# Decoding two cached-attention and MLP layers: the last wo behind the last V, the next K in quarters of chunks, and idle products on TensorE

## The chip, the core and the metric

One core of a Trainium2 chip runs the kernel in one launch. The metric is device time in microseconds (us), the median of several executions. All data is float32, and the caches and weights come from HBM in each execution: 286.14 MB.

## What is computed

One token (D = 512) goes through attention with a cache, an MLP, and both once more with the same weights and caches:

```python
def _A_ref(x, k_cache, v_cache, wq, wo):          # 32 heads, 4096 keys, 128 wide
    q = (x @ wq).reshape(B, Sq, H, Dh).transpose(0, 2, 1, 3)
    scores = jnp.einsum("bhqd,bhkd->bhqk", q, k_cache) * (Dh ** -0.5)
    p = _softmax(scores, axis=-1)
    o = jnp.einsum("bhqk,bhkd->bhqd", p, v_cache)
    return o.transpose(0, 2, 1, 3).reshape(B, Sq, H * Dh) @ wo
def _B_ref(x, w1, b1, w2, b2):                    # F = 1376
    return jnp.einsum("bsf,fd->bsd", _gelu(jnp.einsum("bsd,df->bsf", x, w1) + b1), w2) + b2
x = x + _A_ref(_layernorm(x, axis=-1), A_k_cache, A_v_cache, A_wq, A_wo)
x = x + _B_ref(_layernorm(x, axis=-1), B_w1, B_b1, B_w2, B_b2)
# and these two lines once more
```

## The kernel before

The 32 heads are worked in G = 8 groups of J = 4. A group's K and its V are 8.39 MB each, cut into C = 8 chunks of NC = 2048 elements per partition; a chunk is four quarters of U = 512, one for each head of the group. All of it lives in one array in SBUF, the arena, at places that the code names: A_AT (0), C_AT (8 NC) and B_AT (16 NC) hold a K or a V each (B_AT's last chunk and a half is used otherwise), SHARED (10 U) and PAIR (8 U) hold weights, SCRATCH one tile.

A group runs through these steps. `scores` (L184): TensorE (PE) multiplies the query with the eight chunks of K into pS. `exponentials` (L189): VectorE (DVE) finds the maximum, ScalarE (ACT) does the exponential. `weights` (L200) turns the result, `values` (L214) multiplies with the eight chunks of V into pO, `head_out` (L219) multiplies with wo, and `next_queries` (L301) makes the next group's queries with wq. The layer's norm is folded in, so queries don't wait for it.

Layer 1 takes the groups 0 to 7. Layer 2 goes back from 7 to 0, since the last group's K and V are still in the arena: K of group 7 in C_AT, V of group 7 in A_AT, and 26 of the 32 quarters of group 6's V in B_AT. The other six quarters were copied to PSUM (pK, L328) and are copied back by ACT in the change of layers (L375). Group 6's K is loaded again during that change, into whatever comes free (`begin_k`, L352): one chunk in SHARED, one in PAIR, two in C_AT behind the scores of chunks 0 and 1, four in C_AT behind those of chunks 2 to 5. `pair` (L364), one load of wq for the next group and wo for group 6, takes C_AT + 6 NC to the end of C_AT, wq first. From n = 2 on (L386), `homes` gives each K and V a third of the arena in turn. The V of n = 2 goes to C_AT in two pieces, chunks 0 to 5 and chunks 6 and 7 (L394).

All loads of weights and caches are issued by one queue, SP, in the order of the code (L70), each when the engines are done with what it overwrites. PE's products are kept in the order of the code too (L74). In a layer's last group V comes in four pieces (LAST: chunks 0 to 3, 4 and 5, 6, 7), its wo is loaded ahead of them to PAIR (L321, L393), and w1 and w2 follow in pieces. `mlp` (L240) multiplies with the four rows of w1, does the gelu on DVE and ACT (L254 to L263) and multiplies with the eleven rows of w2 (L264), piece by piece as they land. In the change of layers w1 and w2 share one place, so w2's pieces wait for PE's products with w1; after the last layer they lie in A_AT and wait for nothing there.

Of the kernel before, what the change touches and what calls it, by code (L numbers as in the profile page):

```python
# [17 lines left out]
P = 128  # L18
# [32 lines left out]
def decode_layers(ctx: ExitStack, tc: tile.TileContext, x, k, v, w, w1, b1, w2, b2, out):  # L51
# [5 lines left out]
    def ctile(name, *shape):  # L57
        return const.tile([P, *shape], F32, name=name)
# [6 lines left out]
    def at(first, n):  # L65
        return arena[:, first : first + n]

    def load(first, src):
        t = at(first, src.shape[-1])
        tc.keep_in_program_order(nc.sync.dma_start(t, src))  # L70
        return t

    def matmul(*a, **kw):
        tc.keep_in_program_order(nc.tensor.matmul(*a, **kw))  # L74

    def quarters(first):
        return [at(first + U * j, U) for j in range(4)]

    def part(src, g, a, b):
        return src[g][:, NC * a : NC * b]  # L80

    def of_w(row, i, n):
        return w[row][:, NC * i : NC * (i + n)]

    def by_four(t):
        return t.rearrange("p (j n) -> p j n", j=4)
# [13 lines left out]
    power = ctile("power", 1)  # L100
    nc.gpsimd.memset(power, -0.5)


    pS, pO = (psum.tile([P, 512], F32, name=n) for n in ("pS", "pO"))
    pK = [psum.tile([P, 512], F32, name=f"pK{i}") for i in range(6)]
# [8 lines left out]
    def of_32(t, n, i=0):  # L114
        return t[:, : 32 * n].rearrange("p (c q) -> p c q", q=32)[:, :, i]
# [12 lines left out]
    def turned(src, wide=False):  # L128

        t = work.tile([P, P], F32, name="turned")  # L130
        if wide:
            for j in range(J):
                q = slice(32 * j, 32 * j + 32)
                nc.vector.transpose(t[q], src[q, P * j : P * (j + 1)])  # L134
        else:
            nc.vector.transpose(t, src[:, :P])
        return t

    def set_x(xin0, scale, xin1, queries=True):
        s = small("x_sum")  # L140
        t = x_wide if queries else small("x1", 8)
        if not queries:
            nc.gpsimd.memset(pairs(t)[:, :, 1], 1.0)
        x = pairs(t)[:, :, 0]
        nc.vector.scalar_tensor_tensor(x, xin0, scale, xin1, op0=ALU.mult, op1=ALU.add, accum_out=s)  # L145
        if queries:
            for j in range(1, J):
                nc.gpsimd.tensor_copy(pairs(t[:, 32 * j :])[:, :, 0], x)
        return t, s

    def minus_mean(s, at):
        for j in range(J):
# [31 lines left out]
    def scores(z, c, kt):  # L184
        for j in range(J):
            matmul(pS[32 * j : 32 * j + C, :], z[:, j, C - 1 - c : 2 * C - 1 - c], kt[j],
                   start=(c == 0), stop=(c == C - 1))
# [26 lines left out]
    def values(i, pt, vt, c):  # L214
        for j in range(J):
            matmul(pO[32 * j : 32 * j + 4, :], pt[:, j, c, :], vt[j],
                   start=(i == 0), stop=(i == C - 1))
# [19 lines left out]
                matmul(pO, on[:, d : d + P], wt[:, d, :], start=(d == 0), stop=(d == 3))  # L237
        return of_32(turned(pS) if last else turned(pO, wide=True), 4)

    def mlp(xs, s, w1_t, w2_t, load_w2=None):  # L240
        xb = small("xb", 4)
        nc.gpsimd.tensor_tensor(xb, pairs(xs)[:, :, 0], b2c, op=ALU.add)  # L242
        for c in range(4):
            for j in range(J):
                matmul(pO[32 * j : 32 * j + 2, :FJ], pairs(xs)[:, c, :], w1_t[c][:, FJ * j : FJ * (j + 1)],
                       start=(c == 0), stop=(c == 3))
            if c == 0:
                nm, ss = mean_of(xs, s)
            if c == 1:
                r = rstd_of(ss)  # L250
            if load_w2 and c < 3:
                load_w2(c)
        ht = at(SCRATCH, 32 * FB)
        nc.vector.transpose(ht, pO[:, : 32 * FB])  # L254
        h, u, a, z, t, g = (small(f"gelu_{i}", FB) for i in "huaztg")
        nc.vector.scalar_tensor_tensor(h, of_32(ht, FB, 1), nm, of_32(ht, FB), op0=ALU.mult, op1=ALU.add)
        if load_w2:
            load_w2(3)
        nc.vector.scalar_tensor_tensor(u, h, r, b1c, op0=ALU.mult, op1=ALU.add)
        nc.vector.scalar_tensor_tensor(a, u, 0.044715, u, op0=ALU.mult, op1=ALU.mult)  # L260
        nc.vector.scalar_tensor_tensor(z, a, 1.0, u, op0=ALU.add, op1=ALU.mult)
        nc.scalar.activation(t, z, AF.Tanh, scale=float(np.sqrt(2.0 / np.pi)))
        nc.vector.scalar_tensor_tensor(g, t, 1.0, u, op0=ALU.add, op1=ALU.mult)  # L263
        for c in range(FB):  # L264
            for j in range(J):
                matmul(pS[32 * j : 32 * j + 1, :P], g[:, c : c + 1], w2_t[c][:, P * j : P * (j + 1)],
                       start=(c == 0), stop=(c == FB - 1))
        return of_32(turned(pS), 4), xb

    def load_w1(first, a, b):  # L270
# [2 lines left out]
    def load_w2(first, a, b):  # L273
        load(first + U * a, w2[:, U * a : U * b])

    def in_rows(first, n, rows):
        return [at(first + n * i, n) for i in range(rows)]
# [4 lines left out]
            for c in range(a, b):  # L282
                yield c, quarters(home + NC * c)

    zero = ctile("zero", 4)
    nc.vector.memset(zero, 0.0)
    xs, s = set_x(zero, 1.0, xcol)

    def first_queries(xs, s, wt):
# [24 lines left out]
    for g in range(G):  # L314
        final = g == G - 1
        k_home, v_home = RING[2 * g % 3], RING[(2 * g + 1) % 3]
        for c, t in blocks(k, g, k_home, HALVES if final else ((0, C),)):
            scores(z, c, t)
        pt, rl = weights(exponentials(sc, nsc))
        if final:  # L320
            wo_t = by_four(load(PAIR, of_w(g % 2, g, 1)))  # L321
        for c, t in blocks(v, g, v_home, LAST if final else ((0, C),)):
            values(c, pt, t, c)
            if g == G - 2:
                for j in range(J):
                    i = 4 * c + j - KEPT_V // U
                    if i >= 0:
                        nc.scalar.copy(pK[i], t[j])  # L328
        if final:
            for i in range(3):  # L330
                load_w1(SHARED, i, i + 1)
            own = head_out(rl, wo_t, last=True)
            load_w1(SHARED, 3, 4)
        else:
            pair = load(PAIR, of_w(g % 2, g, 2))
            acc = add_up(acc, head_out(rl, by_four(pair[:, :NC])))
            wq_t = by_four(pair[:, NC:])
            z = next_queries(g + 1, xs, negm, wq_t)
    x1, s1 = set_x(own, 1.0, acc, queries=False)
    own, xb = mlp(x1, s1, in_rows(SHARED, W1C, 4), in_rows(SHARED, U, FB),  # L340
                  lambda i: load_w2(SHARED, *W2_AT_CHANGE[i]))
    xs, s = set_x(own, 0.5, xb)

# [3 lines left out]
    wq_t = by_four(load(SHARED, of_w((g + 1) % 2, g, 1)))  # L349
    k_t = []  # L350

    def begin_k(home, a, b):  # L352
        load(home, part(k, g, a, b))
        k_t.extend(quarters(home + NC * i) for i in range(b - a))

    begin_k(SHARED + NC, 0, 1)
    begin_k(PAIR + NC, 1, 2)
    for c in range(C):
        scores(z, c, quarters(C_AT + NC * c))
        if c == 1:  # L360
            begin_k(C_AT, 2, 4)
        if c == 5:
            begin_k(C_AT + 2 * NC, 4, 8)
    pair = load(C_AT + 6 * NC, of_w(g % 2, g - 1, 2))  # L364
    p = exponentials(sc, nsc)
    z = next_queries(1, xs, negm, wq_t)
    pt, rl = weights(p)
# [2 lines left out]
    acc = add_up(acc, head_out(rl, wo_t))  # L370

    v_t = [at(B_AT + U * i, U) for i in range(KEPT_V // U)]
    for i, first in enumerate([SHARED + 8 * U, SHARED + 9 * U] + [PAIR + U * j for j in range(4)]):
        t = at(first, U)
        nc.scalar.copy(t, pK[i])  # L375
        v_t.append(t)
    for c in range(C):
        scores(z, c, k_t[c])
    pt, rl = weights(exponentials(sc, nsc))
    for c in range(C):  # L380
        values(c, pt, v_t[4 * c : 4 * c + 4], c)
# [4 lines left out]
    for n in range(2, G):  # L386
        g, final = G - 1 - n, n == G - 1
        k_home, v_home = homes[(2 * n - 1) % 3], homes[2 * n % 3]
        for c, t in blocks(k, g, k_home, HALVES if final else ((0, C),)):
            scores(z, c, t)  # L390
        pt, rl = weights(exponentials(sc, nsc))
        if final:
            wo_t = by_four(load(PAIR, of_w(g % 2, g, 1)))  # L393
        for c, t in blocks(v, g, v_home, LAST if final else ((0, 6), (6, 8)) if n == 2 else ((0, C),)):  # L394
            values(c, pt, t, c)
        if final:
            for a, b in HALVES_W1:
                load_w1(A_AT, a, b)
            for a, b in W2_AT_END:
                load_w2(A_AT + 11 * U, a, b)  # L400
            own = head_out(rl, wo_t, last=True)
        else:
            pair = load(PAIR, of_w(g % 2, g - 1, 2))
            acc = add_up(acc, head_out(rl, by_four(pair[:, NC:])))
            z = next_queries(n + 1, xs, negm, by_four(pair[:, :NC]))
    x1, s1 = set_x(own, 1.0, acc, queries=False)
    own, xb = mlp(x1, s1, in_rows(A_AT, W1C, 4), in_rows(A_AT + 11 * U, U, FB))
    y = small("y", 4)
    nc.vector.scalar_tensor_tensor(y, own, 0.5, xb, op0=ALU.mult, op1=ALU.add)
    nc.sync.dma_start(out, y)  # L410
# [42 lines left out]
```

## Time and profile before

| | |
|---|---|
| median of 3 runs | 684.42 us (682.33 to 685.11) |
| the profiled execution | 684.1 us |
| its span, first to last instruction | 681.9 us |
| PE busy | 417.0 us (61%), mean granted clock 0.841 |
| DVE, ACT busy | 110.1 us, 22.2 us |
| read from HBM | 286.14 MB, 420 GB/s over the span |

The profile is of one execution. A row of the timeline gives start, duration, engine, line, operation, what is written and read, and the count; in brackets stands how long the engine was idle before it and what ended that. A product of float32 operands is recorded as two instructions, so x8 of 128x512 are four products. A row of a stretch gives the busy time of PE, PE's weight loads, DVE, ACT and POOL, then the clock that PE was granted (1.00 is full speed), the busy share of the DMA engines and GB/s. A row of DMA issues ends with the us from issue to landing, a median where there are several.

### The profile page before, as it was taken

Reading aid. Unit: us, or ns where it says so; the run is one execution under the profiler, and the core shown is the slowest. Engines: PE = TensorE matmul, PEld = TensorE weight load, DVE = VectorE, ACT = ScalarE, POOL = GpSimd, SP = SyncE. Lnnn points to the kernel's source line nnn. Section 1 sums busy time; section 2 is a strip of 40 time slices with the busy share of each in tenths; the row PEclk is TensorE's granted clock in tenths of the full one; section 3 lists DMA queues with packets and bytes.
Section 4 is the critical chain, followed back from the end, with each engine's and each line's share of the span. In section 5 each row is a group of like instructions: output and inputs, shape, how many; then the busy total and the mean of one; then the engine's idle time right before and its main releaser. Section 6 shows DMA issues by size and latency. Waiting matters only on the chain. (4 is left out here: it accounts for less than half of the span.)

```text
span 681.9 us, 6303 instructions
## 1 busy us (share of the span) xinstructions
PE 417.0 (61%) x2768; PEld 115.8 (17%) x2768; DVE 110.1 (16%) x431; ACT 22.2 (3%) x47; POOL 4.3 (1%) x21
## 2 busy tenths in 40 slices
PE   1536566485564875547656897776456765656755
PEld 0102111021121211112103221221121111211212
DVE  1012101111011111211202212221021101210202
ACT  0010000000000000001000010000000000000000
POOL 1000000000000000000000000000000000000000
PEclk9969878797687876988976898989597876987968
DMA  9999999999999999999999999999999999999996
GB/s 369 432 431 431 439 442 451 432 433 431 428 431 405 454 428 431 431 417 433 430 405 319 354 451 425 399 446 428 443 435 415 455 431 428 431 443 409 428 414 273
DMA packets 10971, 286.54 MB, mean 420 GB/s; under 512 B 1728, under 2 KB 1728, under 8 KB 3008
## 3 DMA queue, kind: packets, MB, share of 16 engines
q1 hardware_dynamic: 10512, 286.14, 98.3%
q8 instruction: 21, 0.34, 0.2%
q10 hardware_dynamic: 432, 0.01, 0.0%
q14 instruction: 6, 0.05, 0.0%
HBM read 286.14 MB, written 0.00 MB: 420 GB/s over the span
## 5 line engine op out<-in xcount | busy, mean ns | idle before, releaser
L74 PE MATMUL pO<-arena,turned 128*4 128x512 f32 x1024 | 143.6, 722 | 91.6 <-DMA arena<-in_v 90.3
L74 PE MATMUL pS<-arena,zq 128*8 128x512 f32 x1024 | 135.1, 687 | 71.9 <-DMA arena<-in_k 66.2
L74 PE MATMUL pO<-arena,x_wide 128*128 128x512 f32 (+1 forms) x176 | 55.7, 533 | 25.1 <-DVE turned L134 18.1
L74 PE MATMUL pO<-arena,on_wide 128*128 128x512 f32 x112 | 51.8, 605 | 18.6 <-DVE on_wide L229 18.6
L74 PEld LDWEIGHTS pO<-arena,turned 128*4 128x4 f32 x1024 | 27.9, 97 | 197.0 <-issue 189.0
L74 PEld LDWEIGHTS pS<-arena,zq 128*8 128x8 f32 x1024 | 28.9, 98 | 174.9 <-issue 165.1
L134 DVE STREAM_TRANSPOSE turned<-pO 32x128 f32<-32x128 f32 x112 | 35.0, 312 | 101.1 <-PE pO L74 99.9
L221 DVE STREAM_TRANSPOSE arena<-pO 128x512 f32<-128x512 f32 x16 | 11.5, 717 | 229.7 <-PE pO L74 229.7
L190 DVE TENSOR_REDUCE ml<-pS 128x1 f32<-128x512 f32 x16 | 11.1, 692 | 183.2 <-PE pS L74 183.2
L202 PE MATMUL pO<-ident,arena 128*128 128x128 f32 x64 | 12.3, 323 | 43.9 <-ACT arena L197 42.4
L74 PEld LDWEIGHTS pO<-arena,x_wide 128*128 128x128 f32 (+1 forms) x176 | 21.8, 160 | 57.8 <-DVE turned L134 26.5
L197 ACT ACTIVATE arena<-pS,mt,sc 128x512 f32<-128x512 f32 x16 | 12.4, 777 | 536.0 <-DVE mt L195 536.0
L74 PEld LDWEIGHTS pO<-arena,on_wide 128*128 128x128 f32 x112 | 20.1, 190 | 51.7 <-DVE on_wide L229 31.6
L202 PEld LDWEIGHTS pO<-ident,arena 128*128 128x128 f32 x64 | 7.9, 159 | 58.5 <-ACT arena L197 51.2
L74 PE MATMUL pS<-arena,gelu_g 128*1 128x128 f32 x176 | 8.1, 329 | 6.8 <-DVE gelu_g L263 4.3
L74 PE MATMUL pO<-arena,x 128*2 128x344 f32 x64 | 7.4, 590 | 1.3 <-DVE x L145 1.3
L74 PEld LDWEIGHTS pS<-arena,gelu_g 128*1 128x1 f32 x176 | 4.3, 94 | 11.2 <-DVE gelu_g L263 5.7
L207 DVE STREAM_TRANSPOSE mt<-ml 128x32 f32<-128x32 f32 x16 | 3.4, 211 | 17.2 <-ACT arena L197 17.2
L74 PE MATMUL pS<-arena,on_wide 128*1 128x128 f32 x64 | 2.9, 344 | 2.6 <-DVE on_wide L227 2.6
L205 DVE COPY turned<-pO 128x128 f32<-128x128 f32 x16 | 4.2, 263 | 1.8 <-PE pO L202 1.8
L242 POOL TENSOR_TENSOR xb<-x,b2c 128x4 f32<-128x4 f32 x2 | 0.4, 198 | 643.3 <-DVE x L145 643.3
L375 ACT COPY arena<-pK 128x512 f32<-128x512 f32 x6 | 3.4, 586 | 20.1 <-issue 13.0
(67 smaller groups left out, 68.6 us busy)
## 6 DMA issues: line engine op xcount, KB each, us to landing
arena<-in_w SPq DMA_DIRECT2D x13, 2048.0 KB, 29.0
arena<-in_k SPq DMA_DIRECT2D x5, 4096.0 KB, 39.2
arena<-in_v SPq DMA_DIRECT2D x2, 4096.0 KB, 19.9
arena<-in_w SPq DMA_DIRECT2D x6, 1024.0 KB, 10.6
arena<-in_v SPq DMA_DIRECT2D x3, 2048.0 KB, 21.2
arena<-in_v SPq DMA_DIRECT2D x1, 6144.0 KB, 26.9
arena<-in_v SPq DMA_DIRECT2D x4, 1024.0 KB, 27.4
arena<-in_w SPq DMA_DIRECT2D x4, 688.0 KB, 30.4
```

The costliest lines, as they stand in the source:

```text
L74: tc.keep_in_program_order(nc.tensor.matmul(*a, **kw))
L134: nc.vector.transpose(t[q], src[q, P * j : P * (j + 1)])
L190: nc.vector.tensor_reduce(ml[:, 0:1], pS, axis=AX.X, op=ALU.max)
L197: nc.scalar.activation(p, pS, AF.Exp, bias=bias[:, 0:1], scale=sc, accum_out=ml[:, 0:1])
L202: tc.keep_in_program_order(nc.tensor.transpose(pT[:, b].rearrange("p j r -> p (j r)"), p[:, P * b : P * (b + 1)], ident))
L205: nc.vector.tensor_copy(pt, pT[:, :, :, :C].rearrange("p b j c -> p j c b"))
L207: nc.vector.transpose(lt, ml)
L221: nc.vector.transpose(ot, pO)
L242: nc.gpsimd.tensor_tensor(xb, pairs(xs)[:, :, 0], b2c, op=ALU.add)
L375: nc.scalar.copy(t, pK[i])
```

## The change

There are three parts.

**The last wo.** In the last group of each layer the load of wo stands behind the four pieces of V instead of ahead of them. In the queue SP, at the end of layer 1 and in the same way at the end of layer 2 (in_w 128x2048 is wo, in_v the pieces of V):

```order
-L70 DMA arena<-in_w 128x2048
 L70 DMA arena<-in_v 128x8192
 L70 DMA arena<-in_v 128x4096
 L70 DMA arena<-in_v 128x2048 x2
+L70 DMA arena<-in_w 128x2048
```

wo moved past four loads of V.

**K in quarters.** In the change of layers, `begin_k` now counts in quarters of chunks. One chunk goes to SHARED and one to PAIR as before; half a chunk goes behind the one in SHARED; C_AT takes one chunk behind the scores of chunk 0, one behind those of chunk 1, and 14 quarters (2 NC to 5.5 NC) behind those of chunk 5. `pair` therefore starts at C_AT + 22 U, half a chunk earlier than before, and the two first copies from pK go to the last two quarters of C_AT instead of SHARED. The places of the V of n = 2 are unchanged. In the queue SP, in the change of layers (in_k is the K of group 6, in_w 128x4096 is `pair`, in_k 128x16384 the K of n = 2):

```order
-L70 DMA arena<-in_k 128x2048 x2
-L70 DMA arena<-in_k 128x4096
-L70 DMA arena<-in_k 128x8192
+L70 DMA arena<-in_k 128x2048
+L70 DMA arena<-in_k 128x1024
+L70 DMA arena<-in_k 128x2048 x3
+L70 DMA arena<-in_k 128x7168
 L70 DMA arena<-in_w 128x4096
 L70 DMA arena<-in_k 128x16384
```

Four loads became six of the same bytes in all; what follows them stands as before.

**Idle products.** `idle` multiplies a column of zeros, taken 128 times as weights, with 512 columns of C_AT, into pS or pO, whose contents are not needed at that point. It stands behind each of the last five chunks of values in a layer's last group, once in each gelu, behind each piece of w2 but the last, and in the change of layers behind the last as well. On PE, around w2 at the end (x_2189 and x_2206 are the MLP's input in the two programs, gelu_g is the gelu's result; x16, x8 and x4 are the products with four rows of w2, two and one):

```order
-L74 MATMUL pO<-arena,x_2189 2x344 x8
-L74 MATMUL pS<-arena,gelu_g 1x128 x44
-L448 UNCONDITIONAL_BRANCH
+L74 MATMUL pO<-arena,x_2206 2x344 x8
+L74 MATMUL pS<-arena,zero 128x512
+L74 MATMUL pS<-arena,gelu_g 1x128 x16
+L74 MATMUL pO<-arena,zero 128x512
+L74 MATMUL pS<-arena,gelu_g 1x128 x16
+L74 MATMUL pO<-arena,zero 128x512
+L74 MATMUL pS<-arena,gelu_g 1x128 x8
+L74 MATMUL pO<-arena,zero 128x512
+L74 MATMUL pS<-arena,gelu_g 1x128 x4
```

The 44 products with w2 stand in four groups now, with one idle product ahead of them and three between them.

The diff:

```diff
--- before.py
+++ after.py
@@ -100,6 +100,9 @@
     power = ctile("power", 1)
     nc.gpsimd.memset(power, -0.5)
 
+    zero = ctile("zero", 4)
+    nc.vector.memset(zero, 0.0)
+
 
     pS, pO = (psum.tile([P, 512], F32, name=n) for n in ("pS", "pO"))
     pK = [psum.tile([P, 512], F32, name=f"pK{i}") for i in range(6)]
@@ -147,6 +150,9 @@
             for j in range(1, J):
                 nc.gpsimd.tensor_copy(pairs(t[:, 32 * j :])[:, :, 0], x)
         return t, s
+
+    def idle(to, n=U):
+        matmul(to[:, :n], zero[:, 0:1].to_broadcast([P, P]), at(C_AT, n), start=True, stop=True)
 
     def minus_mean(s, at):
         for j in range(J):
@@ -237,7 +243,7 @@
                 matmul(pO, on[:, d : d + P], wt[:, d, :], start=(d == 0), stop=(d == 3))
         return of_32(turned(pS) if last else turned(pO, wide=True), 4)
 
-    def mlp(xs, s, w1_t, w2_t, load_w2=None):
+    def mlp(xs, s, w1_t, w2_t, pieces, load_w2=None):
         xb = small("xb", 4)
         nc.gpsimd.tensor_tensor(xb, pairs(xs)[:, :, 0], b2c, op=ALU.add)
         for c in range(4):
@@ -250,6 +256,7 @@
                 r = rstd_of(ss)
             if load_w2 and c < 3:
                 load_w2(c)
+        idle(pS)
         ht = at(SCRATCH, 32 * FB)
         nc.vector.transpose(ht, pO[:, : 32 * FB])
         h, u, a, z, t, g = (small(f"gelu_{i}", FB) for i in "huaztg")
@@ -265,6 +272,10 @@
             for j in range(J):
                 matmul(pS[32 * j : 32 * j + 1, :P], g[:, c : c + 1], w2_t[c][:, P * j : P * (j + 1)],
                        start=(c == 0), stop=(c == FB - 1))
+            if any(c == b - 1 for a, b in pieces[:-1]):
+                idle(pO)
+        if load_w2:
+            idle(pO)
         return of_32(turned(pS), 4), xb
 
     def load_w1(first, a, b):
@@ -282,8 +293,6 @@
             for c in range(a, b):
                 yield c, quarters(home + NC * c)
 
-    zero = ctile("zero", 4)
-    nc.vector.memset(zero, 0.0)
     xs, s = set_x(zero, 1.0, xcol)
 
     def first_queries(xs, s, wt):
@@ -317,16 +326,17 @@
         for c, t in blocks(k, g, k_home, HALVES if final else ((0, C),)):
             scores(z, c, t)
         pt, rl = weights(exponentials(sc, nsc))
-        if final:
-            wo_t = by_four(load(PAIR, of_w(g % 2, g, 1)))
         for c, t in blocks(v, g, v_home, LAST if final else ((0, C),)):
             values(c, pt, t, c)
+            if final and c > 2:
+                idle(pS)
             if g == G - 2:
                 for j in range(J):
                     i = 4 * c + j - KEPT_V // U
                     if i >= 0:
                         nc.scalar.copy(pK[i], t[j])
         if final:
+            wo_t = by_four(load(PAIR, of_w(g % 2, g, 1)))
             for i in range(3):
                 load_w1(SHARED, i, i + 1)
             own = head_out(rl, wo_t, last=True)
@@ -337,9 +347,10 @@
             wq_t = by_four(pair[:, NC:])
             z = next_queries(g + 1, xs, negm, wq_t)
     x1, s1 = set_x(own, 1.0, acc, queries=False)
-    own, xb = mlp(x1, s1, in_rows(SHARED, W1C, 4), in_rows(SHARED, U, FB),
+    own, xb = mlp(x1, s1, in_rows(SHARED, W1C, 4), in_rows(SHARED, U, FB), W2_AT_CHANGE,
                   lambda i: load_w2(SHARED, *W2_AT_CHANGE[i]))
     xs, s = set_x(own, 0.5, xb)
+
 
 
 
@@ -349,19 +360,21 @@
     wq_t = by_four(load(SHARED, of_w((g + 1) % 2, g, 1)))
     k_t = []
 
-    def begin_k(home, a, b):
-        load(home, part(k, g, a, b))
-        k_t.extend(quarters(home + NC * i) for i in range(b - a))
-
-    begin_k(SHARED + NC, 0, 1)
-    begin_k(PAIR + NC, 1, 2)
+    def begin_k(home, n):
+        a = len(k_t)
+        load(home, k[g][:, U * a : U * (a + n)])
+        k_t.extend(at(home + U * i, U) for i in range(n))
+
+    begin_k(SHARED + NC, 4)
+    begin_k(SHARED + 2 * NC, 2)
+    begin_k(PAIR + NC, 4)
     for c in range(C):
         scores(z, c, quarters(C_AT + NC * c))
-        if c == 1:
-            begin_k(C_AT, 2, 4)
+        if c < 2:
+            begin_k(C_AT + NC * c, 4)
         if c == 5:
-            begin_k(C_AT + 2 * NC, 4, 8)
-    pair = load(C_AT + 6 * NC, of_w(g % 2, g - 1, 2))
+            begin_k(C_AT + 2 * NC, 14)
+    pair = load(C_AT + 22 * U, of_w(g % 2, g - 1, 2))
     p = exponentials(sc, nsc)
     z = next_queries(1, xs, negm, wq_t)
     pt, rl = weights(p)
@@ -370,12 +383,12 @@
     acc = add_up(acc, head_out(rl, wo_t))
 
     v_t = [at(B_AT + U * i, U) for i in range(KEPT_V // U)]
-    for i, first in enumerate([SHARED + 8 * U, SHARED + 9 * U] + [PAIR + U * j for j in range(4)]):
+    for i, first in enumerate([C_AT + 30 * U, C_AT + 31 * U] + [PAIR + U * j for j in range(4)]):
         t = at(first, U)
         nc.scalar.copy(t, pK[i])
         v_t.append(t)
     for c in range(C):
-        scores(z, c, k_t[c])
+        scores(z, c, k_t[4 * c : 4 * c + 4])
     pt, rl = weights(exponentials(sc, nsc))
     for c in range(C):
         values(c, pt, v_t[4 * c : 4 * c + 4], c)
@@ -389,11 +402,12 @@
         for c, t in blocks(k, g, k_home, HALVES if final else ((0, C),)):
             scores(z, c, t)
         pt, rl = weights(exponentials(sc, nsc))
+        for c, t in blocks(v, g, v_home, LAST if final else ((0, 6), (6, 8)) if n == 2 else ((0, C),)):
+            values(c, pt, t, c)
+            if final and c > 2:
+                idle(pS)
         if final:
             wo_t = by_four(load(PAIR, of_w(g % 2, g, 1)))
-        for c, t in blocks(v, g, v_home, LAST if final else ((0, 6), (6, 8)) if n == 2 else ((0, C),)):
-            values(c, pt, t, c)
-        if final:
             for a, b in HALVES_W1:
                 load_w1(A_AT, a, b)
             for a, b in W2_AT_END:
@@ -404,7 +418,7 @@
             acc = add_up(acc, head_out(rl, by_four(pair[:, NC:])))
             z = next_queries(n + 1, xs, negm, by_four(pair[:, :NC]))
     x1, s1 = set_x(own, 1.0, acc, queries=False)
-    own, xb = mlp(x1, s1, in_rows(A_AT, W1C, 4), in_rows(A_AT + 11 * U, U, FB))
+    own, xb = mlp(x1, s1, in_rows(A_AT, W1C, 4), in_rows(A_AT + 11 * U, U, FB), W2_AT_END)
     y = small("y", 4)
     nc.vector.scalar_tensor_tensor(y, own, 0.5, xb, op0=ALU.mult, op1=ALU.add)
     nc.sync.dma_start(out, y)
```

## The prediction

> **What bounds the kernel now.** I read the slices of the page first, then busy time by stretches, then the chain that ended last, then the DMA issues and the timeline of SP and PE at the change of layers and at the end. By the stretches DMA is the bound: 286.14 MB have to come in, and the queue is full almost everywhere.
>
> ```profile
> DMA  9999999999999999999999999999999999999996
> 300.00:357.00 57.00, 34.09 (x216) 8.51 (x216) 7.81 (x31) 4.05 (x8) 0.00 (x0) 0.82 0.99 421
> 357.00:386.50 29.50, 22.68 (x283) 8.20 (x284) 6.36 (x35) 1.28 (x3) 1.73 (x6) 0.71 0.89 322
> 386.50:434.00 47.50, 37.52 (x230) 11.04 (x228) 11.46 (x43) 4.08 (x8) 0.00 (x0) 0.96 1.01 431
> 434.00:445.00 11.00, 7.55 (x68) 2.09 (x68) 2.57 (x11) 0.87 (x2) 0.00 (x0) 1.00 0.94 384
> 445.00:675.00 230.00, 143.65 (x890) 38.57 (x892) 37.25 (x142) 4.55 (x11) 0.75 (x2) 0.83 1.00 430
> ```
>
> The last three figures of a row are granted clock, DMA share and GB/s. The one long hole is the change of layers, 357 to 386.5: 322 GB/s against 430, so 29.5 x (1 - 322/430) = 7.4 us of queue time are missing. After 445 the queue never runs dry, so whatever moves the loads that stand there by x us moves the end by x.
>
> ```profile
> 464.64 46.49 DMA arena<-in_k
> ...
> 654.77 22.97 DMA arena<-in_w
> 677.74 0.04 issue
> 677.78 0.62 PE pS L74 x16
> 678.42 0.44 PE pS L74 x8
> 678.89 0.33 DVE turned L136
> 679.24 0.16 DVE y L409
> ```
>
> The chain says the same: loads up to 677.74, then 1.1 us of products of w2 and two DVE steps. Ahead of 464.64 this chain is PE and DVE, from 388 on, because SP waits there for buffers. That is where the change acts.
>
> **The change part by part.**
>
> *Pair's new home.* This decides my forecast. Before, `pair` (wq and wo for the second half of layer 2's turn) lay at C_AT + 6 NC = 24 U, so wq in 24 U to 28 U. Now it starts at 22 U, wq in 22 U to 26 U. The V of n == 2 still goes to C_AT in two pieces, the first 0 to 24 U, the second 24 to 32 U. What a load waits for is shown by the rows of SP and PE:
>
> ```profile
> 398.47 0.33 SPq L70 DMA_DIRECT2D arena<-in_k  x1
> 410.48 0.33 SPq L70 DMA_DIRECT2D arena<-in_v  x1
> 433.10 0.33 SPq L70 DMA_DIRECT2D arena<-in_v  x1
> 433.57 0.34 SPq L70 DMA_DIRECT2D arena<-in_w  x1
> 433.95 0.43 SPq L70 DMA_DIRECT2D arena<-in_k  x1
> 403.36 7.05 PE L74 MATMUL pS<-arena,zq 128*8 128x512 f32 x64
> 429.37 3.70 PE L74 MATMUL pO<-arena,x_wide 128*128 128x512 f32 x8 [1.38 <-DVE turned L134]
> ```
>
> The first V piece left when the scores of g = 6, which read K there, were done (403.36 + 7.05 = 410.41). The second left when the query products that read wq were done (429.37 + 3.70 = 433.07). With wq from 22 U on, the first piece overwrites wq's first two quarters, so it too waits for those products: half of them, 429.37 + 1.85 = 431.2 on before's clock. SP issues in order, so the second piece, the next pair and the K of n == 3 stand behind it.
>
> ```profile
> arena<-in_k SPq DMA_DIRECT2D x1, 24.4
> arena<-in_v SPq DMA_DIRECT2D x1, 6144.0 KB, 26.9
> arena<-in_v SPq DMA_DIRECT2D x1, 2048.0 KB, 9.2
> arena<-in_w SPq DMA_DIRECT2D x1, 688.0 KB, 5.1
> out<-y SPq DMA_DIRECT2D x1, 2.0 KB, 1.4
> ```
>
> These are us from issue to landing. K (398.47) landed at 422.9, the first V piece (410.48) at 437.4, the second (433.10) at 442.3: 14.5 us for 6.29 MB and 4.9 us for 2.10 MB, 433 GB/s, no hole. Now the queue empties after K and stays empty until the first piece is let go. How long an empty queue takes beyond the bytes is bounded by the 2 KB store (1.4 us) and by the 688 KB load of w1 that went out at 357.67 into a nearly empty queue (5.1 less 0.70 MB at 433 GB/s = 3.5 us). I take 2.5. With p for the time by which PE comes to these products sooner, the second V piece lands at 431.2 - p + 2.5 + 14.5 + 4.9 = 453.1 - p, against 442.3: **10.8 - p later**. A page of the Trainium skill (DMA: Bandwidth & Descriptors, Latency and other measured facts) gives about 0.6 us to the first byte for loads issued like these. By that figure, an estimate, the landing would come 1.9 us sooner and the sum would be that much smaller; the rows above, 1.4 us for 2 KB and more for the load, do not go so low.
>
> What makes DMA faster in the change of layers is then worth nothing by itself: it only lengthens the hole ahead of that V. Only p counts.
>
> *How much sooner PE is (p).*
>
> ```profile
> 345.76 8.36 PE L74 MATMUL pO<-arena,turned 128*4 128x512 f32 x56 [6.25 <-DMA arena<-in_v]
> 355.57 1.04 PE L74 MATMUL pO<-arena,turned 128*4 128x512 f32 x8 [1.45 <-DMA arena<-in_v]
> 366.02 0.62 PE L74 MATMUL pS<-arena,gelu_g 128*1 128x128 f32 x16 [2.13 <-DVE gelu_g L263]
> 367.37 1.46 PE L74 MATMUL pS<-arena,gelu_g 128*1 128x128 f32 x24 [0.73 <-DMA arena<-in_w]
> 371.31 1.46 PE L74 MATMUL pS<-arena,gelu_g 128*1 128x128 f32 x24 [0.38 <-DMA arena<-in_w]
> 373.41 1.03 PE L74 MATMUL pO<-arena,x_wide 128*2 128x128 f32 x16 [0.64 <-DVE x_wide L145]
> 376.15 9.07 PE L74 MATMUL pS<-arena,zq 128*8 128x512 f32 x64 [0.71 <-DVE pS L168]
> 385.15 3.70 PE L74 MATMUL pO<-arena,x_wide 128*128 128x512 f32 x8
> 370.00:380.00 10.00, 8.27 (x112) 3.15 (x105) 1.78 (x13) 1.07 (x2) 0.98 (x4) 0.50 0.89 323
> ```
>
> An idle product has the shape of those at 385.15, four in 3.70 us: 0.93 us at full clock, some 1.85 at half (clock 0.50, as in the row from 370 to 380). wo is 1.05 MB, 2.4 us at 433 GB/s, so each V piece lands 2.4 us sooner (the last at 353.1), wo itself where the last V piece landed. Values then start at 343.3; four idle products of 0.93 us stand between the last four chunks of 0.86 us. They end at 355.3 to 357.0, depending on when the clock rises, against 356.6: up to 1.3 sooner, or 0.4 later. The fifth lies beside DVE's turn of pO (1.2 us before on_wide), and costs 0.9 if DVE were not there. The first products of w1 then free their rows up to 2 us sooner, and w2's pieces land about 2 us sooner. Between them PE does 0.35 us, idle, 0.8, idle, 0.8, idle, 0.8 at full clock, 5.5 us against 366.02 to 372.77 = 6.75 before. The idle product in the gelu is hidden under DVE's 2 us there. The one after w2 stands beside DVE's 0.6 us between the last product and 373.41 and costs 0.3. I take the queries 1.5 us sooner, 0.5 more from their own products at full clock, and 2.0 from the scores, which take 7.05 us at full clock (the row at 403.36) instead of 9.07. Sum: **p = 4.0**. Bounds: 5.5 if the values end at 355.3, and -1 if the clock stays at half through w2, so that the idle products eat what the sooner loads give.
>
> K in quarters needs no term: with a load let go by w2's products 8 and 9, by the queries and by the scores of chunks 0, 1 and 5, the queue is full, and all K lands by about 391, ahead of its scores. If it did not, those would wait as before. The copies of the first two kept quarters now wait for the last scores instead of w2's products:
>
> ```profile
> 372.03 1.07 ACT L375 COPY arena<-pK 128x512 f32<-128x512 f32 x2 [6.26 <-PE pS L74]
> 387.04 0.78 ACT L197 ACTIVATE arena<-pS,mt,sc 128x512 f32<-128x512 f32 x1 [13.94 <-DVE mt L195]
> ```
>
> They stand ahead of the exponentials on ACT, 1.07 us in the 1.8 us that DVE takes after the scores (385.22 to 387.04): nothing; without that cover, 1.1.
>
> So V lands 10.8 - 4.0 = **6.8 us later**, and the end with it.
>
> *The end.* The order of wo and V changes no byte ahead of w2's last piece. V comes 2.4 us sooner, but PE meets idle products there too, so the gelu is done at the same time or 0.7 us sooner, relative to the loads.
>
> ```profile
> 674.97 1.06 PE L74 MATMUL pS<-arena,gelu_g 128*1 128x128 f32 x32 [2.20 <-DVE gelu_g L263]
> 676.53 1.06 PE L74 MATMUL pS<-arena,gelu_g 128*1 128x128 f32 x32 [0.51 <-DMA arena<-in_w]
> 677.78 1.04 PE L74 MATMUL pS<-arena,gelu_g 128*1 128x128 f32 x24 [0.19 <-DMA arena<-in_w]
> ```
>
> Three idle products, 2.8 us, go between these groups, whose waits for DMA are 0.51 and 0.19 us: 0.7 is hidden, 2.1 is not. With the gelu sooner, 1.6. I take **1.8**; the ends are 0, if the last piece lands late enough, and 3.5 at half clock. The Trainium skill (TensorE: Matmul & The Clock Gate, Back-to-back issue gap) puts a lone product of 512 columns at 216 ns at full clock. By that figure the three would cost 0.65 us, all hidden, and the sum would be 1.8 us less; the row at 385.15, with this kernel's type, says 0.93 us for one.
>
> *Sum.* The profiled execution took 684.1 us for a span of 681.9; 684.1 + 6.8 + 1.8 = 692.7. The median of the runs is 684.42, 0.3 more, so I forecast **693.0**.
>
> **The rivals.**
>
> 1. *PE gains nothing.* The idle products keep PE busy but at half clock, and take from w2 what the sooner loads give: p = 0. For it: in the row 370 to 380 PE is busy 8.27 of 10 us and still at 0.50. Against: with the idle products its gaps there are gone. 684.4 + 10.8 + 1.8 = 697.0. Chance 0.15.
> 2. *The idle products at the end are hidden*, because w2's last pieces come late against PE: 684.4 + 6.8 + 0.2 = 691.4. For it: 22.97 us of loads end the chain. Against: PE is held for only 0.7 us there. Chance 0.13.
> 3. *The V of n == 2 is not held back*, and the time falls. This needs its first piece in the queue before K has landed, about 416 after a refilled change of layers, that is issued by 413; it decides there. Then the queue keeps most of the 7.4 us, until the second piece, free at 433.1 - 4.0 = 429.1, lands at 429.1 + 2.5 + 4.9 = 436.5, 5.8 sooner than 442.3: 684.4 - 5.8 + 1.8 = 680.4. For it: the hole in the change is real. Against: 22 U to 24 U lie in both, and the issue at 433.10 shows that such a load waits. Chance 0.05, which also holds the case that the two cancel.
>
> **How the numbers follow.** The forecast case has the remaining 0.67: 693.0, from 690 to 696 with p from 1 to 5.5 and the end from 0.8 to 3. The range 689.0 to 697.5 takes it with rivals 1 and 2, and leaves out rival 3 and the outer ends of p. A measurement of this kernel can tell about 0.5%, 3.4 us. Slower by more holds in all cases but rival 3: 0.91. Rival 3 is shared out as 0.04 faster and, with a hole half as long as I reckon, 0.05 within.
>
> **What would show it.** Right: SP issues the first V piece after K of n == 2 near 427 instead of 410.48, just as the x_wide products end, and the second piece, pair and K directly after it; DMA moves next to nothing for 10 us or more before; the change of layers runs near 430 GB/s; scores there take about 7 us; three 128x512 products stand between w2's pieces ahead of the end. Wrong: the first V piece issued while scores of g = 6 end, no hole between 410 and 430, or a last w2 product right behind its load.

## The result and the profile after

| | before | after |
|---|---|---|
| median of 6 runs | 684.38 us (682.21 to 685.60) | 694.55 us (693.40 to 695.17) |
| ratio to before | | 1.0153 (95% interval 1.0132 to 1.0174) |
| the profiled execution, its span | 684.1, 681.9 us | 694.56, 692.8 us |

The kernel is 10.2 us slower by the medians and 10.9 us by the spans. The page shows where at a glance. These are the slices of after, each 17.3 us wide:

```profile
DMA  9999999999999999999999993999999999999995
GB/s 401 444 424 420 425 431 429 447 440 424 425 428 439 440 443 421 424 420 432 417 351 376 457 435 108 410 462 431 425 428 428 447 435 429 431 429 416 429 419 226
```

The hole of the change of layers (slices 21 and 22, 351 and 376 GB/s) is still there, and there is a new one, the 25th slice with 108 GB/s. By stretches (the last three figures are granted clock, DMA share and GB/s):

```profile
357.00:380.00 23.00, 19.07 (x272) 6.95 (x274) 5.35 (x31) 0.21 (x1) 1.73 (x6) 1.00 0.91 338
380.00:414.00 34.00, 27.67 (x192) 8.03 (x188) 9.16 (x35) 5.15 (x10) 0.00 (x0) 0.97 1.03 440
414.00:429.00 15.00, 12.30 (x66) 3.92 (x59) 2.54 (x8) 0.00 (x0) 0.00 (x0) 0.96 0.20 84
429.00:445.00 16.00, 8.97 (x71) 2.26 (x70) 3.99 (x16) 0.87 (x2) 0.00 (x0) 0.92 0.98 399
445.00:686.00 241.00, 152.02 (x938) 41.07 (x942) 36.83 (x138) 4.55 (x11) 0.75 (x2) 0.83 1.00 428
```

The DMA now runs at 440 GB/s from 380 on, where before had its hole until 386.5, and then does almost nothing from 414 to 429. What it waits for is in the rows of SP and PE, and in the issues of K and the two V pieces with the us to their landing:

```profile
395.67 0.33 SPq L70 DMA_DIRECT2D arena<-in_k  x1
428.58 2.10 SPq L70 DMA_DIRECT2D arena<-in_v  x2
430.80 0.38 SPq L70 DMA_DIRECT2D arena<-in_w  x1
431.21 0.46 SPq L70 DMA_DIRECT2D arena<-in_k  x1
426.56 3.70 PE L74 MATMUL pO<-arena,x_wide 128*128 128x512 f32 x8 [1.38 <-DVE turned L137]
arena<-in_k SPq DMA_DIRECT2D x1, 24.7
arena<-in_v SPq DMA_DIRECT2D x1, 6144.0 KB, 17.8
arena<-in_v SPq DMA_DIRECT2D x1, 2048.0 KB, 20.9
```

K (395.67) landed at 420.4. The first V piece left at 428.58, when half of the products with wq were done (426.56 + 1.85 = 428.41), 18.1 us later than before (410.48). It landed at 446.4, and the second piece, issued at the end of the two that the second row merges (428.58 + 2.10 - 0.33 = 430.35), at 451.2 instead of 442.3. The second piece, the next pair and the K of n = 3 stood behind the first piece, but their issues (430.35, 430.80 and 431.21) are no later than before: there they left at 433.10, 433.57 and 433.95, some 2.7 us later. What is lost is the time in which the first piece could have moved. From there on the queue is full (428 GB/s), and those 8.9 us are still there at w2's last piece, issued at 668.57 in after and at 659.67 in before:

```profile
668.57 0.33 SPq L70 DMA_DIRECT2D arena<-in_w  x1
arena<-in_w SPq DMA_DIRECT2D x1, 256.0 KB, 18.4
659.67 0.33 SPq L70 DMA_DIRECT2D arena<-in_w  x1
arena<-in_w SPq DMA_DIRECT2D x1, 256.0 KB, 18.7
```

It landed at 687.0 against 678.4, 8.6 us later. The other part is behind that landing. The chain of after ends with:

```profile
683.75 1.05 PE pS L74 x32
684.80 1.05 PE pO L74 x2
685.86 0.99 PE pS L74 x32
686.84 1.05 PE pO L74 x2
687.90 0.55 PE pS L74 x16
688.45 1.05 PE pO L74 x2
689.50 0.38 PE pS L74 x8
```

The rows of pO x2 are the idle products, 1.05 us each. PE never waits for w2 here; it ends at 689.88, 2.9 us after the last landing, where before ended 0.5 us after it (678.86 against 678.4). So 8.6 + 2.4 = 11.0 us, against 10.9 us between the spans.

### The profile page after: what moved, and what is told of

The parts are those of the page before. It is cut to its first block, busy times and chain, and to the rows that moved or that the text cites. A ratio compares the mean times of both kernels' runs of the same rounds, so it can differ in the third digit from the quotient of the medians.

```text
span 692.8 us, 6386 instructions
## 1 busy us (share of the span) xinstructions
PE 432.1 (62%) x2806; PEld 119.4 (17%) x2806; DVE 110.3 (16%) x431; ACT 22.2 (3%) x47; POOL 4.3 (1%) x21
## 5 line engine op out<-in xcount | busy, mean ns | idle before, releaser
L74 PE MATMUL pO<-arena,x_wide 128*128 128x512 f32 (+1 forms) x176 | 54.9, 509 | 24.2 <-DVE turned L137 18.1
L74 PE MATMUL pO<-arena,on_wide 128*128 128x512 f32 x112 | 51.8, 605 | 19.5 <-DVE on_wide L235 17.3
L74 PE MATMUL pS<-arena,zero 128*128 128x512 f32 x24 | 13.5, 644 | 0.0
L74 PE MATMUL pS<-arena,gelu_g 128*1 128x128 f32 x176 | 6.3, 272 | 3.3 <-DVE gelu_g L270 2.2
L74 PE MATMUL pO<-arena,zero 128*128 128x512 f32 x14 | 7.9, 644 | 0.0
L74 PE MATMUL pO<-arena,x 128*2 128x344 f32 x64 | 5.7, 451 | 2.6 <-DMA arena<-in_w 1.4
L74 PEld LDWEIGHTS pS<-arena,zero 128*128 128x128 f32 x24 | 3.6, 186 | 9.8 <-issue 9.8
## 6 DMA issues: line engine op xcount, KB each, us to landing
arena<-in_v SPq DMA_DIRECT2D x1, 6144.0 KB, 17.8
```

## The experiments

The theory: the place of wq holds back V, and that costs about 9 us; the idle products at the end cost about 2.4; the rest of the change is worth little. The rivals: (A) the small loads of K and the later wo cost the time; (B) the idle products cost it. Each kernel was timed beside the kernel before on its own chip, so ratios are compared, not times.

**V cut at another place.** In the changed kernel:

```diff
-((0, 6), (6, 8)) if n == 2
+((0, 5), (5, 8)) if n == 2
```

> The changed kernel, but the V of n = 2 comes in chunks 0 to 4 and 5 to 7 instead of 0 to 5 and 6 to 7, so that its first piece (0 to 20 U) no longer overlaps the new place of wq (22 U to 26 U). Theory (the first V piece is held back by the readers of wq): it is issued when the scores of g = 6 end, near 407.6 instead of 428.6, the hole between K and V goes, and the second piece (3.1 MB), issued at 428.6, lands near 439.5 instead of 451.2; about 11 to 12 us less, so 682 to 684 us. Rival A (the small quarters of K and the late wo cost the time): unchanged within 2 us, near 694. Rival B (the idle products cost it all over the kernel): near 694 too.

Ratio 1.0017 (0.9998 to 1.0035), 684.29 us; the profile's span is 682.2 us, 10.6 less than after. The hole is gone, and SP lets the first V piece go at 408.25. From this kernel, the stretch of the hole and the queue's rows with the landings:

```profile
414.00:429.00 15.00, 12.29 (x69) 3.67 (x62) 2.54 (x8) 0.00 (x0) 0.00 (x0) 0.96 0.96 413
408.25 22.90 SPq L70 DMA_DIRECT2D arena<-in_v  x2
arena<-in_v SPq DMA_DIRECT2D x1, 5120.0 KB, 25.2
arena<-in_v SPq DMA_DIRECT2D x1, 3072.0 KB, 9.8
```

The second piece landed at 440.6 (issued at 430.8). The ratio is 0.0136 lower than with the overlap of half a chunk, 9.3 us, and 9.9 us lower than in the repetition of after that follows below. Rivals A and B fall as explanations of the 9 us.

**The same wait put into the kernel before:**

```diff
-((0, 6), (6, 8)) if n == 2
+((0, 7), (7, 8)) if n == 2
```

> The kernel before with one edit: the V of n = 2 comes in chunks 0 to 6 and 7, so that its first piece overlaps wq (24 U to 28 U) there too. Nothing else of the change is in it. Theory: the first piece waits until 433.1 for the products with wq, lands 20.3 us later at 453.3 and the second at 455.8 against 442.3 before: 13.4 us more, near 697.8. Rivals A and B (small quarters, idle products): no change, 684.4.

Ratio 1.0201 (1.0162 to 1.0239), 13.7 us where 13.4 was expected. Its profile shows the same hole, with nothing of the change in the program:

```profile
414.00:429.00 15.00, 12.30 (x68) 3.79 (x61) 2.54 (x8) 0.00 (x0) 0.00 (x0) 0.93 0.23 100
431.07 0.80 SPq L70 DMA_DIRECT2D arena<-in_v  x2
427.34 3.70 PE L74 MATMUL pO<-arena,x_wide 128*128 128x512 f32 x8 [1.38 <-DVE turned L134]
arena<-in_v SPq DMA_DIRECT2D x1, 7168.0 KB, 21.0
```

The piece leaves when the products end (427.34 + 3.70 = 431.04). The two runs show the cause from both sides.

**No idle products at all**, in the changed kernel:

```diff
 def idle(to, n=U):
-    matmul(to[:, :n], zero[:, 0:1].to_broadcast([P, P]), at(C_AT, n), start=True, stop=True)
+    pass
```

> The changed kernel with no idle product at all. Theory: the end gets 2.4 us back; in the change of layers the scores of g = 7 and the queries run at half clock again (2.0 and 0.8 us lost), which the sooner end of the values (by 2 us, without four idle products) makes good for a part: the V of n = 2 leaves between 428 and 431, so 691.5 to 694.5. Rival B (the idle products cost the time): near 685.

Ratio 1.0143 (1.0105 to 1.0180), within the theory's 1.010 to 1.015 and not rival B's. V left at 431.31, just beyond the 428 to 431 that I had expected: the scores of g = 7 took 9.38 us and not 7.05, and the granted clock from 357 to 380 was 0.57. The profiled execution was the longest of the four (696.20 us; the others took 691.46 to 693.27).

```profile
375.78 9.38 PE L74 MATMUL pS<-arena,zq 128*8 128x512 f32 x64 [0.71 <-DVE pS L174]
431.31 0.33 SPq L70 DMA_DIRECT2D arena<-in_v  x1
```

**No idle products between w2's pieces at the end**, in the changed kernel:

```diff
-            if any(c == b - 1 for a, b in pieces[:-1]):
+            if load_w2 and any(c == b - 1 for a, b in pieces[:-1]):
```

> The changed kernel without the three idle products between w2's pieces after the last layer; those in the change of layers stay. Theory (three products of 1.05 us, of which 0.7 lie beside waits for w2): 2.4 us less than the changed kernel, 692.1. Rival (PE is ahead of w2's last pieces anyway, the end is bound by their landing): no change, 694.5.

Ratio 1.0135 (1.0107 to 1.0163). The end of its chain shows that PE ends 0.5 us behind its loads again (at 688.03, w2's last piece landed at 687.52):

```profile
666.63 20.27 DMA arena<-in_w
686.91 0.04 issue
686.95 0.62 PE pS L74 x16
687.57 0.02 issue
687.59 0.44 PE pS L74 x8
```

By the ratios it is 1.2 us under after, or 1.8 under the repetition of after that follows; the intervals overlap, so the size isn't settled by this pair.

**The changed kernel once more**, on the same chip as the next kernel, the idle products alone and the quarters alone.

> The changed kernel as it is, for comparison on the same chip. Every theory expects the ratio to before that it showed, 1.015.

Ratio 1.0162 (1.0136 to 1.0188).

**Both edits together:** V cut at 5, and no idle products between w2's pieces at the end.

> The changed kernel with both edits: the V of n = 2 in chunks 0 to 4 and 5 to 7, and no idle products between w2's pieces after the last layer. Theory: the hole ahead of V (10.5 us in the profiles) and the end's 2.4 us are independent and both go: 694.5 - 10.5 - 2.4 = 681.6, a ratio to before of about 0.997. Rival (the idle products at the end only fill time that a colder clock would take): the same as with the V edit alone, ratio 1.002.

Ratio 0.9976 (0.9958 to 0.9994), as the theory has it: 2.8 us under the V edit alone, and the intervals don't overlap.

**The parts of the change alone, on the kernel before.** First all idle products at the places of the change, with the loads as before:

```diff
+        idle(pS)
...
+            if any(c == b - 1 for a, b in pieces[:-1]):
+                idle(pO)
+        if load_w2:
+            idle(pO)
...
+            if final and c > 2:
+                idle(pS)
```

Then K in quarters as the change has it, with V cut at 5, no idle products and wo ahead of V:

```diff
+    begin_k(SHARED + NC, 4)
+    begin_k(SHARED + 2 * NC, 2)
+    begin_k(PAIR + NC, 4)
...
+    pair = load(C_AT + 22 * U, of_w(g % 2, g - 1, 2))
...
-((0, 6), (6, 8)) if n == 2
+((0, 5), (5, 8)) if n == 2
```

Then wo alone, moved behind V in both layers:

```diff
-        if final:
-            wo_t = by_four(load(PAIR, of_w(g % 2, g, 1)))
         for c, t in blocks(v, g, v_home, ...
...
+            wo_t = by_four(load(PAIR, of_w(g % 2, g, 1)))
```

> The kernel before with the idle products alone; wo, K and pair as before. Theory: no load is held back, so only the end's 2.4 us are seen, less what the change of layers gains from the clock, 0 to 1 us: 1.5 to 2.5 us over before, ratio 1.002 to 1.004. Rival B (idle products cost along the whole kernel, or explain the 10 us): ratio over 1.01. Rival C (the clock that they keep up pays for them): ratio 1.000 or less.

> The kernel before with the K of group 6 in quarters, pair at 22 U and the V of n = 2 in chunks 0 to 4 and 5 to 7; no idle products, wo ahead of V as before. Theory: the finer loads fill 1 to 2 us of the hole in the change of layers and nothing waits longer, so 1 to 2 us under before, ratio 0.997 to 0.999. Rival A (small loads are slow and cost more than they fill): ratio 1.003 or more.

> The kernel before with wo behind V in both layers and nothing else. Theory: V and what follows it on PE come 2.4 us sooner, but the end waits for w2's last piece and the change of layers for w1's fourth row, whose places in the queue did not move: no change, ratio 0.998 to 1.001. Rival (values are on the path to the end): up to 2.4 us less at each layer's end, ratio 0.994.

The idle products alone: 1.0071 (1.0046 to 1.0096), 4.9 us, twice what I expected, though not rival B's 10. Quarters alone: 1.0003 (0.9986 to 1.0021), no change where I expected 1 to 2 us less. wo alone: 0.9984 (0.9966 to 1.0002), as expected. Why the idle products cost more alone: with wo ahead of V, V lands later than in the changed kernel (the values of layer 1 begin at 345.52 against 343.19), and the products between the pieces push the last values from 356.6 to 359.0 in the change of layers. At the end of layer 2 it is the same: the chain runs back from the gelu over the last values and the idle products between them, without a wait for w1. From the kernel with idle products alone, the last values of layer 1 and the end of the chain:

```profile
357.97 1.04 PE L74 MATMUL pO<-arena,turned 128*4 128x512 f32 x8
676.59 1.05 PE pS L74 x32
677.64 1.05 PE pO L74 x2
682.34 0.37 PE pS L74 x8
```

The products with w2 begin at 676.59 and end at 682.71, against 674.97 and 678.86 before: 1.6 us come from the values and 2.2 from the products between w2's pieces, as much as the spans differ (685.8 and 681.9). In the changed kernel the values of layer 1 end at 356.7, as before, so there the later wo pays for the products between the V pieces.

**The three idle products at the end alone**, on the kernel before:

```diff
+            if not load_w2 and any(c == b - 1 for a, b in pieces[:-1]):
+                idle(pO)
```

> The kernel before with the three idle products between w2's pieces at the end of layer 2 alone. Theory: 3 x 1.05 less 0.7 of waits, 2.4 us more, ratio 1.0035. Rival (all of the 4.6 us that the idle products cost together come from here): ratio 1.007.

Ratio 1.0004 (0.9985 to 1.0023): **no change, where the theory expected 1.0035**. Its one profile does show the products on the path: w2 runs from 673.06 to 680.77, 4.5 us beyond the landing of w2's last piece (676.28).

**No idle products between V pieces**, V cut at 5, with and without the three at the end:

```diff
-            if final and c > 2:
-                idle(pS)
```

> The changed kernel with the V of n = 2 in chunks 0 to 4 and 5 to 7, without idle products between w2's pieces at the end and without those between the last V pieces in both layers; those in both gelus and between w2's pieces in the change of layers stay. Theory: the idle products between V pieces take what the late wo gives PE, but neither end hangs on that, so the same as with them, ratio to before 0.996 to 0.999. Rival (values are on the path): 1 to 2 us less, ratio 0.995 or below; or, if the clock falls in w1 and w2 without them, 1 us more.

> The last kernel (V of n = 2 in chunks 0 to 4 and 5 to 7, no idle products between the V pieces) with the three idle products between w2's pieces at the end put back. Theory (they delay the end by 2.4 us whatever stands ahead of them): ratio to before 0.9958 + 0.0035 = 0.999. Rival (without idle products between V pieces ahead of them they cost nothing on average, as in the kernel before): 0.996.

Without the three: 0.9958 (0.9939 to 0.9977), **681.23 us, the best kernel here**, 0.42% under before. That is just under the 0.996 to 0.999 of the theory, and the interval holds the rival's 0.995 too. With the products between V pieces the ratio was 0.9976 (0.9958 to 0.9994), so what they cost isn't settled. With the three at the end: 1.0017 (0.9997 to 1.0038), above the theory's 0.999 and the rival's 0.996. Here the three cost 4.0 us by the ratios, about 2 to 6 by the two intervals, so the 2.4 that their place in the chain gives is possible and nothing at all is not. In the kernel before they cost -1.0 to 1.6 us, which excludes the 2.4. One thing that bears on it: kernels without idle products don't always end at full clock. In the stretch of the last products with w2, the kernel before, the one with quarters alone and the one with wo alone (PE busy after the width; granted clock third from the end):

```profile
675.00:679.00 4.00, 3.10 (x88) 1.84 (x88) 0.11 (x1) 0.00 (x0) 0.00 (x0) 1.00 0.31 121
```

```profile
675.00:680.00 5.00, 4.25 (x88) 3.10 (x88) 0.54 (x3) 0.00 (x0) 0.00 (x0) 0.66 0.15 58
```

```profile
675.00:680.00 5.00, 4.06 (x88) 2.71 (x88) 0.50 (x3) 0.21 (x1) 0.00 (x0) 0.64 0.08 31
```

The same 88 products took 3.10 us at a clock of 1.00, and 4.25 and 4.06 us at 0.66 and 0.64. So an end at the lower clock loses time without any idle product. Counted from the landing of w2's last piece to the end of the last product with w2, the profiles give:

| kernels | granted clock in the last 4 us | us from that landing to the end |
|---|---|---|
| without the three: before, V cut at 7, no products at the end, both edits, no products between V pieces | 1.00 | 0.50 to 0.53 |
| without the three: no idle products at all, wo alone, quarters alone | 0.57 to 0.63 | 1.75 to 2.53 |
| with the three: after, its repetition, V cut at 5 | 1.00 | 2.77 to 2.92 |
| with the three: idle products alone, the three alone, and put back with no products between V pieces | 0.99 to 1.00 | 4.03 to 5.00 |

Against an end at full clock the three products of after cost 2.4 us; against an end at the lower clock they would cost as little as 0.2 (2.77 - 2.53). The timed runs also show that the kernel before depends on its clock: of its 86 executions beside these kernels, on three chips, the 38 with a mean granted clock of 0.835 or less took 685.25 us (median), the 29 with 0.840 or more took 682.66. So the three products would cost little on average in a kernel that often ends at the lower clock. That this is why they cost nothing in the kernel before isn't shown: there is one profile of each kernel, and its end with the three products (4.49 us) is among the long ones. The question stays open.

## Why the prediction was right, and where its sizes were off

The forecast was 693.0 us, slower, and 694.55 was measured. The spans were forecast to differ by 6.8 + 1.8 = 8.6 us and differ by 10.9: the way and the mechanism were right, and both terms of the sum were too small. The steps, against the profile:

- **The first V piece waits for the products with wq, and the queue runs empty.** Right, shown by the rows at 428.58 and 426.56, by the V edit (the hole goes) and by the kernel before with a longer first piece (the hole comes). The loads behind that piece stood behind it, as forecast, but left 2.7 us sooner than before; the time is lost in the empty queue.
- **What DMA gains in the change of layers only lengthens that hole.** Right: 440 GB/s from 380 on, then 84. With the hole taken away the change of layers gives little as well: quarters alone gave 1.0003.
- **The sum at V**, 10.8 - p with p = 4.0, forecast 6.8 us later; it was 8.9. Two terms were off. The queue took 17.8 us for 14.5 us of bytes, 3.3 and not 2.5 beyond them. The 0.6 us to the first byte of the Trainium skill (DMA: Bandwidth & Descriptors, Latency and other measured facts), taken as the estimate took it for all the time beyond the bytes, is further off than my 2.5; no row here shows the first byte by itself. And p was 2.8 (431.2 - 428.4).
- **p itself.** This is the term that I mis-sized, at "I take the queries 1.5 us sooner". PE in the change of layers, after:

```profile
343.19 5.39 PE L74 MATMUL pO<-arena,turned 128*4 128x512 f32 x32 [3.54 <-DMA arena<-in_v]
355.65 1.04 PE L74 MATMUL pO<-arena,turned 128*4 128x512 f32 x8
362.24 0.76 PE L74 MATMUL pO<-arena,x 128*2 128x344 f32 x8 [0.28 <-DMA arena<-in_w]
365.14 0.62 PE L74 MATMUL pS<-arena,gelu_g 128*1 128x128 f32 x16 [1.08 <-DVE gelu_g L270]
367.62 0.84 PE L74 MATMUL pS<-arena,gelu_g 128*1 128x128 f32 x24 [0.81 <-DMA arena<-in_w]
371.60 0.84 PE L74 MATMUL pS<-arena,gelu_g 128*1 128x128 f32 x24 [0.21 <-DMA arena<-in_w]
373.42 0.62 PE L74 MATMUL pO<-arena,x_wide 128*2 128x128 f32 x16
375.39 7.05 PE L74 MATMUL pS<-arena,zq 128*8 128x512 f32 x64 [0.48 <-DVE pS L174]
```

The values began 2.6 us sooner and ended at 356.7, as in before (356.6): the idle products took it all. The pieces of w2 were still awaited at 367.62 and 371.60 (367.37 and 371.31 before), so my "about 2 us sooner" for them was wrong, and the queries began at 373.42 against 373.41. The other two parts came as forecast: the queries' own products 0.8 us (0.5 forecast), the scores 2.0. That the idle products cause the 2.0 is likely, and not shown run by run: in all eight profiles with idle products in the change of layers these scores took 7.05 us; of the six without, three have 7.05 too (V cut at 7, quarters alone, the three at the end alone) and the others 9.07 (before), 8.48 (wo alone) and 9.38 (no idle products). So a part of p is chance, that of the execution of the kernel before that was profiled. The kernel before with the longer V piece has the same program up to that load, and its products with wq began at 427.34, 2.0 us sooner than before's; against it p is 427.34 - 426.56 = 0.8.

- **The end**, forecast 1.8, was 2.4 in the profile: three products of 1.05 us where each stands between other products, not the 0.93 of one among its like. Of their 3.15 us 0.7 was hidden, as forecast: the waits of 0.51 and 0.19 are gone. The gelu was not sooner, for which I had taken 0.3 off; w2's products begin 3.2 us ahead of the last landing (683.75 and 686.97), and began 3.4 ahead of it before (674.97 and 678.37). The 216 ns that the Trainium skill gives for a lone product of 512 columns (TensorE: Matmul & The Clock Gate, Back-to-back issue gap) does not hold for these: the rows say 1.05 us for a product, which is recorded as two instructions. On average over runs the size is less sure: taking the three out gave 1.2 to 2.8 us in the changed kernel and with V cut at 5, 4.0 in one pair, and putting them into the kernel before gave none.
- **The rivals.** V not held back (rival 3) is refuted. Its price of 680.4 us, a ratio of 0.994, was too hopeful for the V edit, which gave 1.0017, but that edit is not quite its case: the second piece is 3.15 MB there and not 2.10, 2.4 us more, and it left at 430.8 and not at 429.1. So it landed at 440.6 where rival 3 had 436.5, 1.7 us sooner than before, and the idle products at the end cost more than that. PE gaining nothing (rival 1) was nearer than I gave it: p was halfway between its 0 and bound of 5.5. The idle products hidden at the end (rival 2) is refuted for this kernel by its chain.

## What to carry to other kernels

When a buffer moves, list who overwrites its new place, not only who reads it: half a chunk of overlap made one load wait 18 us for the readers of another, and the queue, which issues in order, ran empty. A stall filled ahead of that wait was worth nothing here. Work put on an idle engine to keep its clock up can cost its full time where the next piece has already landed, as at the end of the changed kernel; look there first, and time it over many runs, since profiles and runs did not agree on its price here.

## What I had not expected

- The empty queue took 3.3 us beyond the bytes of a 6.29 MB load (17.8 against 14.5).
- The same three idle products cost nothing that can be measured in one kernel (1.0004, 0.9985 to 1.0023) and 4.0 us, about 2 to 6, in another (1.0017 against 0.9958). Open.
- K in finer loads fills a visible hole in DMA (the stretch from 380 on) and leaves the time as it was (quarters alone, 1.0003).
